# Copying x's pieces on GpSimd and taking more products straight from PSUM, in a fused long convolution and spectral mixing kernel

## The chip, the cores and the metric

The kernel runs on one core of a Trainium2 chip. A core has five engines with a queue of instructions each: TensorE for matmuls (PE in the profile, with its weight loads apart as PEld), VectorE (DVE), ScalarE (ACT), GpSimd (POOL) and SyncE (SP), which here only issues transfers. Each engine works through its own queue in order; engines wait for one another by semaphores. Matmuls write to PSUM, eight banks of 512 float32 a partition; DVE and ACT carry results from there to the on-chip memory SBUF. Transfers to and from DRAM are issued by SP or by GpSimd and done by 16 DMA engines.

The metric is the time of one execution in microseconds (us) on the device, the median of several runs. Lower is better.

## The reference

Two layers, one after the other, on x of shape (8, 5696, 128): batch, sequence, channels.

```python
# layer 1: causal long convolution along the sequence, by FFT
L = 2 * S
y = irfft(rfft(x, n=L, axis=1) * rfft(h, n=L, axis=0)[None], n=L, axis=1)[:, :S]
# layer 2: 64 Fourier modes of y, mixed over channels by a complex matrix per mode
X = rfft(y, axis=1)[:, :64]
Yr = einsum('bmd,mde->bme', X.real, w_r) - einsum('bmd,mde->bme', X.imag, w_i)
Yi = einsum('bmd,mde->bme', X.real, w_i) + einsum('bmd,mde->bme', X.imag, w_r)
u = y + irfft(Yr + 1j * Yi, n=S, axis=1)     # the other modes are zero
out = u + relu(u @ w_ch)
```

Inputs and output are float32; the kernel works in float16 with float32 sums in PSUM.

## The kernel before

The transforms are matmuls with fixed matrices. The sequence of 5696 is split as 89 x 64 (`NQ`, `J`). The batch is taken as four **pairs** of two; `g_` (0 to 3) counts them.

**Where x comes in.** A pair's x comes in eight pieces (`i`, 0 to 7: four for each batch entry). `x_load` issues two transfers for a piece from GpSimd's queue; they turn float32 into float16 and land in a staging tile, `Xr` for pair 0 and `Xt` for the others. `x_place` then copies the piece on DVE into `Xin` (L356), whose rows of 128 numbers stand 130 apart: 89 partitions, 16 rows of 128. `Xt` lies over the front of `As`, of which ticks already done are free.

**First transform.** `a_tile` j (0 to 31) multiplies four columns of `Xin` by the matrix `F` and evacuates the result into `As`, on DVE (L314) or ACT (L310). It needs all eight pieces. Tiles 0 to 5 of the next pair are done in the last ticks of the present one (table `border`), the rest between pairs. In that stretch GpSimd also issues the `wscr` transfers, which rearrange the mixing weights in DRAM.

**Ticks.** There are 90 frequencies, four to a tick, so 23 ticks (t = 0 to 22) a pair, and three more in which later steps run out. At each tick:

- `second`: 16 matmuls of `As` by `M` give the spectrum of x in two PSUM banks, one for each batch entry. `slot_of` says which of two slots of two banks. In pairs 1 to 3 the matmuls of an odd tick and of the next even one stand together (`twin`).
- `products`: DVE multiplies the spectrum by the spectrum of h, in `Hs`, into one of three `U` buffers (L592). In most ticks ACT first copies the spectrum from PSUM to `Xs` (`copied`, L308) and DVE reads `Xs`; in **straight** ticks DVE reads PSUM itself and there is no copy. Before the change the straight ticks are t = 3, 7, 11, 15, 19 of pairs 1 to 3; tick 0 has a form of its own (L584).
- Two ticks later four matmuls of `U` by `Wc` give Z; ACT casts it to `Zs` or `Zt`, two casts a tick (L308), and SP sends it to DRAM (`zscr`).
- A tick after that, eight matmuls of Z by `G` add to the 64 modes of layer 2.

In pair 0 the ticks to t = 16 also make the spectrum of h for tick t + 6 (`filter_tick`): matmuls, an evacuation to `Hs` on DVE (L312), and two transfers from SP that bring its halves to the other partitions.

**What sets the order.** Every instruction is recorded in the order in which the Python code calls for it; `Recorder` derives the waits from the tokens that an instruction reads and writes. There is no other planner, so an engine's queue is the order of the calls. At each tick `tick` calls first `x_place` for the pieces that the table `XPLACE` names, then `second` and `products`, then at even ticks 2 to 16 `x_load` of piece t/2 - 1 of the next pair (after the product of that tick), then the U matmuls, the casts and the G matmuls. The pieces are placed at ticks 9, 10, 12, 15, 16, 18, 20, 22 of pair 0 and 9, 10, 13, 14, 17, 18, 20, 22 of pairs 1 and 2, all on DVE.

**After the pairs** the modes are mixed (weights `W`), and the last stage, about a third of the time, brings convolution and modes back to the sequence (`UT`), multiplies by `w_ch` and writes the output. `reflect` (L505 on DVE) fills the second half of two of its matrices, `S4a` and `IBs`; memsets on GpSimd (L493) clear parts of the tiles that Z comes back to.

Of the kernel before, what the change touches and what calls it, by code (L numbers as in the profile page):

```python
# [7 lines left out]
U32 = mybir.dt.uint32  # L8
# [115 lines left out]
def bass_long_conv_fft__then__afno_spectral_mix_kernel(nc, x, h, moe_w_r, moe_w_i, moe_w_ch, out):  # L124
    B, S, D = x.shape
# [3 lines left out]
    NQ = S // J  # L129
# [3 lines left out]
    NP = B // 2  # L133
# [72 lines left out]
    def at(name, cols, dt, off):  # L206
        return nc.alloc_sbuf_tensor_at(name, [P, cols], dt, offset=off)
# [10 lines left out]
    XS = D + 2  # L218
    XW = 2 * J * XS
    a_x = take(XW * 2)  # L220
    x_sb = at("Xin", XW, F16, a_x)
# [7 lines left out]
    NU, NXS, NZ, NZX = 3, 2, 6, 10  # L229
# [8 lines left out]
    XN = J // XC  # L238
    XB = XN * D
    x_raw = [at(f"Xr{i}", XB, F16, a_h + 2 * XB * i) for i in range(2 * XC)]  # L240
    x_st = [at(f"Xt{i}", XB, F16, a_as + i * XB * 2) for i in range(2 * XC)]
    u_s = [at(f"U{i}", 2048, F16, a_st + i * 4096) for i in range(NU)]
    x_s = [at(f"Xs{i}", 1024, F16, a_st + NU * 4096 + i * 2048) for i in range(NXS)]
    z_s = [at(f"Zs{i}", 1024, F16, a_st + NU * 4096 + (NXS + i) * 2048) for i in range(NZ)] + \
# [47 lines left out]
    R = Recorder(nc)  # L292
# [39 lines left out]
    def turns(name, items):  # L332
        i = ring2.get(name, 0)
        ring2[name] = i + 1
        return items[i % len(items)]
# [19 lines left out]
    def x_place(i, src, toks):  # L355
        R.add("vector", lambda e: e.tensor_copy(bass.AP(x_sb, i * XN * XS, [[XW, NQ], [XS, XN], [1, D]]),  # L356
                                                bass.AP(src, 0, [[XB, NQ], [D, XN], [1, D]])),
              list(toks) + XZ, [("xin", i)])

    def w_pieces():  # L360
# [13 lines left out]
    XZ = [("xz",)]  # L374
# [20 lines left out]
    XSLOT = [0, 2]  # L395
# [13 lines left out]
    for j in range(16):  # L409
        t = turns("h", [0, 2, 4])  # L410
# [126 lines left out]
    def with_h_at(g_, t):  # L537
        return g_ == 0 and t + LH < NT
# [3 lines left out]
    def copied(g_, t, sl):  # L542
        n = len(ticks[t])
        e = onchip[(g_, t)] = turns("e", list(range(NXS)))
        evac(bass.AP(x_s[e], 0, [[1024, P], [512, 2], [1, n * D]]), pv(sl, 0, [[512, 2], [1, n * D]]), [bank(sl), bank(sl + 1)],
             [("xs", e)], eng="scalar")
        return e

    def twin(g_, t):
        return g_ > 0 and t % 2 == 1  # L550

    def straight(g_, t):
        return g_ > 0 and t % 4 == 3

    def slot_of(g_, t):
        if g_ == 0 or t == 0:
            return XSLOT[(t + 1) % 2 if t and not with_h_at(g_, t) else 0]
        return XSLOT[((t - 1) // 4 + t) % 2]

    def second(g_, t):  # L560
        sl = slot_of(g_, t)
        for i, k in enumerate(ticks[t]):
            for r in range(2):
                for b in range(2):
                    col = k * 3 * J + (J if r == 0 else 0) + b * J
                    mm(pv(sl + b, i * D, [[1, D]]),
                       ap(m_sb, MW, J * b, J, col, [[1, P]]),
                       ap(a_sb, AW, J * b, J, (2 * k + r) * D, [[1, D]]), r == 0, r == 1,
                       AST + mtok(k), [bank(sl + b)])

    def products(g_, t, sl):
        n = len(ticks[t])
        bk = [bank(sl), bank(sl + 1)]
        i = t % NU
        hv = bass.AP(h_sb, KT * t * D, [[2 * HW, P], [HW, 2], [0, 2], [1, n * D]])
        uv = bass.AP(u_s[i], 0, [[2048, P], [1024, 2], [512, 2], [1, n * D]])
        src = pv(sl, 0, [[0, 2], [512, 2], [1, n * D]])
        if t == 0:
            e = turns("e", list(range(NXS)))
            evac(bass.AP(x_s[e], 512, [[1024, P], [1, n * D]]), pv(sl + 1, 0, [[1, n * D]]), [bank(sl + 1)], [("xs", e)], eng="scalar")  # L580
            hv = bass.AP(h_sb, 0, [[2 * HW, P], [HW, 2], [1, n * D]])
            for b, s_, tok, done in ((0, pv(sl, 0, [[0, 2], [1, n * D]]), bank(sl), ("u", i)),
                                     (1, bass.AP(x_s[e], 512, [[1024, P], [0, 2], [1, n * D]]), ("xs", e), ("u0", i))):
                R.add("vector", lambda e, b=b, s_=s_: e.tensor_tensor(bass.AP(u_s[i], b * 512, [[2048, P], [1024, 2], [1, n * D]]), s_, hv, MULT),  # L584
                      [tok, ("h", t, 0), ("h", t, 1, 0), ("h", t, 1, J)], [done])
            return
        if not straight(g_, t):
            e = onchip.get((g_, t))
            if e is None:
                e = copied(g_, t, sl)  # L590
            src, bk = bass.AP(x_s[e], 0, [[1024, P], [0, 2], [512, 2], [1, n * D]]), [("xs", e)]
        R.add("vector", lambda e: e.tensor_tensor(uv, src, hv, MULT),  # L592
              bk + [("h", t, 0), ("h", t, 1, 0), ("h", t, 1, J)], [("u", i)])

    Z_OLD = [("ag", k) for k in range(NS, NS + 8 * (NZX - NZ))]
    XPLACE = [9, 10, 12, 15, 16, 18, 20, 22], [9, 10, 13, 14, 17, 18, 20, 22]

    def zroom(g_, s_):
        return (s_ - 2 * NZ) % NZX if g_ == 0 and s_ >= 2 * NZ else s_ % NZS[g_]

    def xtok(n):
        return [("xt", n, p_) for p_ in range(2)]

    def tick(g_, t):
        if g_ + 1 < NP:
            for i in range(2 * XC):
                if t == XPLACE[g_ > 0][i]:
                    x_place(i, x_st[i], xtok(i))
        with_h = with_h_at(g_, t)
        if t < NT:  # L610
            of_two = t > 0 and twin(g_, t - 1)
            if not of_two:
                second(g_, t)
            products(g_, t, slot_of(g_, t))
            if twin(g_, t):
                second(g_, t + 1)
                if straight(g_, t):
                    copied(g_, t + 1, slot_of(g_, t + 1))
        drain = list(border[t]) if t in border and g_ + 1 < NP else []
        if drain and t >= NT:  # L620
            j, sl, e = drain.pop(0)
            a_tile(j, [sl], e)
        if g_ + 1 < NP and t % 2 == 0 and 0 < t <= 4 * XC:
            i = t // 2 - 1
            x_load(g_ + 1, i, x_st[i], xtok(i), [("u", t % NU)] + AST)
        if LC <= t < NT + LC:
            s_ = t - LC
            n = len(ticks[s_])
            i, zi = s_ % NU, zroom(g_, s_)
            zb = [turns("z", ZBANK) for b in range(2)]  # L630
            for b in range(2):
                for r in range(2):
                    mm(pv(zb[b], 0, [[1, n * D]]), (W1, W2)[r], u_s[i][:, r * 1024 + b * 512:r * 1024 + b * 512 + n * D],
                       r == 0, r == 1, [("u", i), ("wc",)] + ([("u0", i)] if s_ == 0 and b else []), [bank(zb[b])])
                evac(bass.AP(z_s[zi], b * D, [[1024, P], [2 * D, n], [1, D]]),
                     pv(zb[b], 0, [[D, n], [1, D]]), [bank(zb[b])], [("zs", zi, b)], eng="scalar",
                     after=once(("zx", zi, b), Z_OLD) if zi >= NZ else ())
            zo = (g_ * NK + KT * s_) * P * 256
            dma("sync", bass.AP(zs, zo, [[256, P], [P * 256, n], [1, 256]]),
                bass.AP(z_s[zi], 0, [[1024, P], [256, n], [1, 256]]), "z",  # L640
                [("zs", zi, 0), ("zs", zi, 1)], [("zd", g_, s_)])
            if drain and t >= NT:
                j, sl, e = drain.pop(0)
                a_tile(j, [sl], e)
        if LM <= t < NT + LM:
            s_ = t - LM
            zi = zroom(g_, s_)
            for b in range(2):
                for i, k in sorted(enumerate(ticks[s_]), key=lambda q: (s_ > 0 or q[1] != 1, q)):
                    if k % 2:  # L650
                        o, off, n, sl = pv(MB, b * P, [[1, P]]), (k + 1) // 2 * P, P, (k + 1) // 2
                    else:
                        ms, off = even[k]
                        n, sl = 2 * len(ms), 0
                        dims = [[M, 2]] if len(ms) == 1 else [[ms[1] - ms[0], 2], [M, 2]]
                        o = pv(MB, b * P + ms[0], dims)
                    mm(o, z_s[zi][:, i * 256 + b * P:i * 256 + b * P + P], g_sb[:, off:off + n],
                       k == 1 and b == 0, k == NK - 1 and b == 1, [("g", sl // GP), ("zs", zi, b)], [bank(MB)])
        if drain and t < NT + LM - 1:
            j, sl, e = drain.pop(0)  # L660
            a_tile(j, [sl], e)
        if with_h:
            filter_tick(t + LH, [2, 3])
# [167 lines left out]
    for g_ in range(NP):  # L831
        last = g_ == NP - 1
        order = [(c_, b) for b in range(2) for c_ in range(NCH)] if last else [(c_, b) for c_ in range(NCH) for b in range(2)]
        for n, (c_, b) in enumerate(order):
            i = NCH * g_ + c_
# [44 lines left out]
```

## Time and profile before

| | |
|---|---|
| median of 3 runs (lowest, highest) | 387.9 us (386.63, 389.21) |
| span of the profiled execution, first to last instruction | 383.2 us |
| what lies around that span, by the median | 4.7 us |
| granted TensorE clock | 0.995 of full speed |
| PE busy | 364.4 us, 95% of the span |
| DVE busy | 312.2 us, 81% |
| ACT busy | 302.2 us, 79% |
| POOL busy | 83.0 us, 22% |

The profile is of one execution; its own time is given as the span alone. The ticks of pair 0 lie at about 45 to 94 us, of pair 1 at 110 to 149, of pair 2 at 166 to 204, of pair 3 at 221 to 260; the stretches between are the first transform of the next pair.

Busy time counts from an instruction's start to its end. Neighbours on an engine overlap by some 0.08 us, so the spacing of starts tells more than durations. A matmul's end is modelled; its start is not. A wait is put down to the event that came last before the instruction; where that engine had long been done, it was another.

### The profile page before, as it was taken

The page shows a single profiled execution, that of the slowest core. Times are in us where ns is not written, and L with a number is a line of the kernel's source. Part 1 is how long each engine was busy: PE and PEld are TensorE (multiplying, and loading weights), DVE is VectorE, ACT ScalarE, POOL GpSimd, SP SyncE. Part 2 cuts the span into 40 slices and gives each one's busy share as a digit, 9 for nine tenths or more (in the row PEclk, how much of TensorE's full clock was granted, in tenths as well). Part 3 has the DMA queues.
Part 4 walks back from the last instruction along what each step waited for, and adds up shares of the span by engine and source line. Part 5 has one row for each costly group of instructions (what it writes and reads, how often), then busy time and mean ns, then how long its engine had stood idle before and what let it go on. Part 6 is the DMA issues. An engine that isn't in the chain of part 4 may idle for free.

```text
span 383.2 us, 12579 instructions
## 1 busy us (share of the span) xinstructions
PE 364.4 (95%) x5396; PEld 284.9 (74%) x5396; DVE 312.2 (81%) x349; ACT 302.2 (79%) x486; POOL 83.0 (22%) x133
## 2 busy tenths in 40 slices
PE   7999999998989999989998989999999999999994
PEld 7997766665866666866666856668898988988873
DVE  6878888997998999998998987885437677767876
ACT  1268689898889997989997989996457676777785
POOL 8400013220453320643220511219400000000000
PEclk9999999999999999999999999999899999999999
DMA  7998559999699999899996839999999999999978
GB/s 147 197 284 329 142 107 268 282 239 296 93 138 198 216 249 252 93 133 198 257 248 193 87 113 364 328 357 388 404 400 398 406 417 401 409 415 380 376 290 355
DMA packets 86865, 103.94 MB, mean 271 GB/s; under 512 B 22638, under 2 KB 72430, under 8 KB 83330
## 3 DMA queue, kind: packets, MB, share of 16 engines
q1 hardware_dynamic: 62523, 67.73, 50.6%
q0 software_dynamic: 24288, 35.43, 43.9%
q8 instruction: 42, 0.69, 0.7%
q14 instruction: 12, 0.10, 0.1%
HBM read 70.61 MB, written 51.12 MB: 318 GB/s over the span
## 4 chain that ended last, share of the span: by engine, by line
PE 73%; DMA 10%; DVE 6%; ACT 5%; POOL 3%; issue 2%; SPq 0%; DVEq 0%; POOLq 0%
PE ps L320 73%; DMA Xr<-in_x_dram 4%; DMA Xt<-in_x_dram 4%; DVE As L314 2%; POOL Xr L317 2%; ACT As L310 2%; DVE U L584 1%; ACT R L814 1%; DMA Hs<-Hs 1%; ACT UT L308 1%; DVE Xin L356 1%; ACT Zs L308 1%; DVE UT L312 0%; DVE O L815 0%; DVE Hs L312 0%
## 5 line engine op out<-in xcount | busy, mean ns | idle before, releaser
L592 DVE TENSOR_TENSOR U<-Xs,Hs 128x2048 f16<-128x2048 f16 (+1 forms) x73 | 86.7, 1191 | 14.3 <-ACT Xs L308 11.2
L320 PE MATMUL ps<-U,Wc 128*128 128x512 f16 (+1 forms) x368 | 94.0, 376 | 0.6 <-DVE U L592 0.6
L308 ACT CAST Xs<-ps 128x1024 f16<-128x1024 f32 (+1 forms) x77 | 74.8, 976 | 11.3 <-PE ps L320 8.7
L308 ACT CAST Zs<-ps 128x512 f16<-128x512 f32 (+1 forms) x134 | 70.6, 596 | 2.7 <-PE ps L320 2.3
L815 DVE TENSOR_TENSOR O<-ps,R 128x512 f32<-128x512 f32 x81 | 52.5, 685 | 19.8 <-ACT R L814 13.1
L314 DVE TENSOR_SCALAR As<-ps 128x720 f16<-128x720 f32 x70 | 58.1, 885 | 5.8 <-PE ps L320 5.0
L814 ACT ACTIVATE R<-ps 128x512 f32<-128x512 f32 x96 | 50.9, 572 | 14.5 <-PE ps L320 14.1
L320 PE MATMUL ps<-F,Xin 128*128 128x180 f16 x512 | 53.9, 250 | 4.2 <-DVE Xin L356 1.7
L320 PEld LDWEIGHTS ps<-F,Xin 128*128 128x128 f16 x512 | 44.5, 155 | 12.8 <-DVE As L314 3.7
L320 PE MATMUL ps<-As,M 64*128 64x128 f16 x1440 | 50.4, 217 | 3.5 <-DVE U L584 2.9
L310 ACT ACTIVATE As<-ps 128x720 f16<-128x720 f32 (+1 forms) x61 | 45.8, 770 | 8.7 <-PE ps L320 7.2
L320 PE MATMUL ps<-WI,UT 128*128 128x256 f16 x360 | 51.7, 278 | 0.5 <-DVE O L815 0.4
L320 PEld LDWEIGHTS ps<-U,Wc 128*128 128x128 f16 x368 | 28.5, 97 | 29.4 <-ACT Zs L308 4.7
L317 POOL DMA_DIRECT2D Xt<-in_x_dram x48 | 25.9, 545 | 104.6 <-PE ps L320 100.7
L320 PEld LDWEIGHTS ps<-As,M 64*128 64x128 f16 x1440 | 40.6, 94 | 8.8 <-DVE U L584 3.6
L308 ACT CAST UT<-ps 128x712 f16<-128x712 f32 x40 | 30.0, 752 | 17.2 <-PE ps L320 16.2
L320 PEld LDWEIGHTS ps<-WI,UT 128*128 128x128 f16 x360 | 39.2, 152 | 4.1 <-issue 1.9
L320 PE MATMUL ps<-IBs,C 128*128 128x356 f16 x128 | 39.7, 319 | 0.8 <-ACT UT L308 0.3
L320 PEld LDWEIGHTS ps<-G,Zs 128*128 128x128 f16 x524 | 28.9, 96 | 14.0
L592 DVE TENSOR_TENSOR U<-ps,Hs 128x2048 f16<-128x2048 f32 x15 | 34.2, 2283 | 0.0
L320 PE MATMUL ps<-G,Zs 128*128 128x128 f16 (+2 forms) x524 | 32.4, 191 | 0.0
L320 PE MATMUL ps<-F 128*128 128x180 f16 x284 | 28.2, 255 | 2.6 <-DMA F<-cF 2.6
(87 smaller groups left out, 506.0 us busy)
## 6 DMA issues: line engine op xcount, KB each, us to landing
out_dram<-O SPq DMA_DIRECT2D x39, 512.0 KB, 10.8
zscr<-Zs SPq DMA_DIRECT2D x64, 256.0 KB, 6.9
Xt<-in_x_dram POOLq DMA_DIRECT2D x24, 320.0 KB, 7.0
zscr<-Zt SPq DMA_DIRECT2D x24, 256.0 KB, 7.2
W<-wscr POOLq DMA_DIRECT2D x4, 1024.0 KB, 8.3
M<-cM POOLq DMA_DIRECT2D x5, 720.0 KB, 20.5
ZT0a<-zscr SPq DMA_DIRECT2D x3, 1024.0 KB, 13.5
Hs<-Hs SPq DMA_DIRECT2D x44, 64.0 KB, 5.4
```

The lines of the kernel that those rows point to most:

```text
L308: R.add(e, lambda h_: h_.copy(dst, src), reads, writes, after=after)
L310: R.add(e, lambda h_: h_.activation(dst, src, COPY, scale=scale), reads, writes, after=after)
L314: R.add(e, lambda h_: h_.tensor_scalar_mul(dst, src, scale), reads, writes, after=after)
L317: R.add(eng, lambda h_: h_.dma_start(dst, src), reads, writes, ring=ring, after=after)
L320: R.add("tensor", lambda h_: h_.matmul(o, l, r, start=st, stop=sp), reads, writes)
L356: R.add("vector", lambda e: e.tensor_copy(bass.AP(x_sb, i * XN * XS, [[XW, NQ], [XS, XN], [1, D]]), bass.AP(src, 0, [[XB, NQ], [D, XN], [1 ...
L584: R.add("vector", lambda e, b=b, s_=s_: e.tensor_tensor(bass.AP(u_s[i], b * 512, [[2048, P], [1024, 2], [1, n * D]]), s_, hv, MULT), [tok, ...
L592: R.add("vector", lambda e: e.tensor_tensor(uv, src, hv, MULT), bk + [("h", t, 0), ("h", t, 1, 0), ("h", t, 1, J)], [("u", i)])
L814: R.add("scalar", lambda e: e.activation(rv, src_r, RELU), bk, [("r", i % NR)], after=once(("r", i % NR), G_ALL + XTT + [("y", 0), ("y", 1 ...
L815: R.add("vector", lambda e: e.tensor_tensor(ov, src_u, rv, ADD), bk + [("r", i % NR)], [key + (h_,)], after=once(key, old))
```

## The change

Two things. First, 20 of the 24 copies from `Xt` to `Xin` move from DVE to GpSimd: the last four of pair 0 and all eight of pairs 1 and 2. They copy the same bytes as 32-bit words, 64 to a row instead of 128 halves. They stand at straight ticks, two to a tick, and wait, beside the piece's landing, for the product of the tick before (the token `("u", (t - 1) % NU)`). Second, the straight ticks become a table: 17, 19 and 21 in pair 0, which had none, and 3, 5, 9, 11, 15, 17, 19, 21 in pairs 1 to 3. `slot_of` counts PSUM slots by the new table. TensorE's and SP's instructions and their order stay; ACT loses 12 of its `Xs` copies.

```diff
+    x_32 = x_sb[:, :].bitcast(U32).tensor
+    xt_32 = [t_[:, :].bitcast(U32).tensor for t_ in x_st]
...
+    def x_place32(i, toks):
+        R.add("gpsimd", lambda e: e.tensor_copy(bass.AP(x_32, i * XN * XS // 2, [[XW // 2, NQ], [XS // 2, XN], [1, D // 2]]),
+                                                bass.AP(xt_32[i], 0, [[XB // 2, NQ], [D // 2, XN], [1, D // 2]])),
+              list(toks) + XZ, [("xin", i)])
...
+    STRAIGHT = [(17, 19, 21)] + [(3, 5, 9, 11, 15, 17, 19, 21)] * (NP - 1)
+
     def straight(g_, t):
-        return g_ > 0 and t % 4 == 3
+        return t in STRAIGHT[g_]
...
     def slot_of(g_, t):
         if g_ == 0 or t == 0:
             return XSLOT[(t + 1) % 2 if t and not with_h_at(g_, t) else 0]
-        return XSLOT[((t - 1) // 4 + t) % 2]
+        n = 1
+        for i in range(2, t + 1):
+            n ^= not straight(g_, i - 2)
+        return XSLOT[n]
...
-    XPLACE = [9, 10, 12, 15, 16, 18, 20, 22], [9, 10, 13, 14, 17, 18, 20, 22]
+    XPLACE = [9, 10, 12, 15, 17, 17, 21, 21], [11, 11, 15, 15, 17, 17, 21, 21]
...
                 if t == XPLACE[g_ > 0][i]:
-                    x_place(i, x_st[i], xtok(i))
+                    if straight(g_, t):
+                        x_place32(i, xtok(i) + [("u", (t - 1) % NU)])
+                    else:
+                        x_place(i, x_st[i], xtok(i))
```

## The prediction

> **What bounds the kernel now.** I read the costliest groups first, for the price of what is moved, then busy time by stretch, to see which engine has room, then the timelines of single engines, for what PE really waits for. Of each group: count, busy time, mean ns of one, idle time before it and its releaser.
>
> ```profile
> L592 DVE TENSOR_TENSOR U<-Xs,Hs 128x2048 f16<-128x2048 f16 (+1 forms) x73 | 86.7, 1191 | 14.3 <-ACT Xs L308 11.2
> L308 ACT CAST Xs<-ps 128x1024 f16<-128x1024 f32 (+1 forms) x77 | 74.8, 976 | 11.3 <-PE ps L320 8.7
> L592 DVE TENSOR_TENSOR U<-ps,Hs 128x2048 f16<-128x2048 f32 x15 | 34.2, 2283 | 0.0
> ```
> ```profile
> L356 DVE COPY Xin<-Xt 89x2048 f16<-89x2048 f16 x24 | 16.4, 682 | 0.8 <-DMA Xt<-in_x_dram 0.8
> ```
>
> A product from PSUM saves ACT a copy and costs DVE about twice as much. Starts follow closer than durations: in the timeline a straight product holds DVE for 2.20 us, one from Xs for 1.14, a placing copy for 0.60.
>
> Next, four ticks of pair 2 (two copies on DVE) and of pair 3 (none); the columns are the stretch, its length, then busy time of PE, PEld, DVE, ACT and POOL.
>
> ```profile
> 180.00:187.00 7.00, 7.00 (x118) 4.63 (x114) 6.89 (x7) 6.89 (x12) 2.08 (x4) 1.00 1.04 214
> 235.00:242.00 7.00, 7.00 (x120) 4.63 (x116) 5.78 (x5) 6.89 (x12) 0.53 (x1) 1.00 1.09 395
> ```
>
> Without the copies DVE is 1.1 us less busy, and the four ticks still take 7.0 us. So DVE is not the bound. ACT at 6.89 could be, or PE. PE's timeline in pair 3 decides it:
>
> ```profile
> 231.05 1.07 PE L320 MATMUL ps<-As,M 64*128 64x128 f16 x32
> ...
> 233.25 1.07 PE L320 MATMUL ps<-U,Wc 128*128 128x512 f16 x4
> ...
> 234.58 1.07 PE L320 MATMUL ps<-As,M 64*128 64x128 f16 x32
> ...
> 236.78 1.02 PE L320 MATMUL ps<-U,Wc 128*128 128x512 f16 x4
> ...
> 238.06 1.07 PE L320 MATMUL ps<-As,M 64*128 64x128 f16 x32
> ```
>
> Two ticks take 3.53 us, the next two 3.48. The first holds PE's only wait (1.07 against 1.02: a weight load waits for ACT's Zs); in the second matmuls follow without a gap. **PE is the bound**, and ACT costs it 0.05 us in four ticks: five times a pair, 0.25 us a pair.
>
> The larger waits lie where a pair ends:
>
> ```profile
> 138.25 1.21 DVE L592 TENSOR_TENSOR U<-Xs,Hs 128x2048 f16<-128x2048 f16 x1
> ...
> 148.18 0.69 DVE L356 COPY Xin<-Xt 89x2048 f16<-89x2048 f16 x1 [0.17 <-DMA Xt<-in_x_dram]
> ```
> ```profile
> 140.00 1.04 POOL L317 DMA_DIRECT2D Xt<-in_x_dram  x2 [2.29 <-PE ps L320]
> ```
> ```profile
> 148.93 0.85 PE L320 MATMUL ps<-F,Xin 128*128 128x180 f16 x8 [0.64 <-DVE Xin L356]
> ```
>
> Tick 16's product ends at 139.46, GpSimd issues piece 7 0.54 later (the PE named as releaser was long done), it lands at about 148.15, DVE copies it, and PE has waited 0.64 us. Pair 2 shows 0.65 in the same place and pair 0 0.40.
>
> **The change, part by part.** It moves 4 + 8 + 8 copies of pairs 0, 1 and 2 to GpSimd and makes 3 products of each pair straight, 12 in all. *ACT* loses 12 Xs copies of 0.98, 11.8 us. This is worth PE's 0.05 us waits alone: at most 0.25 in each of three pairs. *DVE* loses 20 copies of 0.60, 12.0 us, and gains 12 times 2.20 - 1.14, 12.7 us. Where straight and copied products alternate, two ticks take DVE 2.20 + 1.14 = 3.34 of PE's 3.48: it fits, with 0.1 to spare, and ticks 7 and 13, copied ones, give back 1.1 each. *PSUM*: a straight product keeps its banks 2.20 us; they are written again 3.48 us later, so nothing waits there.
>
> *GpSimd* gains 20 copies of 1024 words, which no row shows. Its memsets of 2048 words take 1.82, so 0.91 for writing as many; that is my nearest row. From below, DVE's own copy at 0.68; from above, 1.82, if a word read and written costs twice a word written. I take 0.95. By the Trainium skill (GPSIMD Engine Reference, "Performance versus the Vector engine") simple bodies take 1.03 cycles a word at 1.2 GHz, an estimate of 0.88, but its measured tight loop 1.8, an estimate of 1.54; the first leaves my sum, the second would give about 398.
>
> *When the copies run.* They wait for the product of the tick before, so as to lie beside the straight one. But in GpSimd's queue the pieces 4, 6 and 7, issued after the products of ticks 10, 14 and 16, stand right ahead of the copies of ticks 11, 15 and 17. Each takes 0.53 to start and 1.04 for its two transfers. So these copies start 1.57 after the straight product and end at 1.57 + 1.90 = 3.47, and the product ends at 2.20. The rest, 1.27, lies beside the next product, from Xs and Hs. Only the copies of tick 21 have no load ahead and fit. What such an overlap costs, the nearest rows show, DVE's and then GpSimd's:
>
> ```profile
> 262.30 3.61 DVE L505 TENSOR_SCALAR S4a<-S4a,SG 128x2759 f16<-128x2759 f16 x1
> ...
> 269.40 0.93 DVE L505 TENSOR_SCALAR IBs<-IBs,SG 128x2759 f16<-128x2759 f16 x1
> ```
> ```profile
> 261.60 1.82 POOL L493 MEMSET ZT1b<- 32x2048 uint32 x1
> 263.35 1.82 POOL L493 MEMSET ZT2b<- 32x2048 uint32 x1
> ```
>
> The same DVE instruction takes 0.93 alone and 3.61 beside two memsets: it ends 0.74 after the second, and did not get in between them. A product from Xs and Hs is no such instruction, so its cost lies between 0 and the whole 1.27; I take 1.27, since it too works from SBUF to SBUF. The Trainium skill (SBUF — State Buffer, "Who interferes with whom") says that a DVE instruction with two SBUF inputs contends with a GpSimd one that reads SBUF, and one with a single SBUF input does not. By that rule the next product is held and the straight one is free; by a reading of the row in which only that kind of instruction is held, the sum would be 386.3. No product in this trace meets a GpSimd read.
>
> *The sum for pairs 1 and 2.* Let e be the end of tick 17's first matmuls (138.4 in pair 1). Unhindered, DVE ends product 16 at e - 0.1. Between a straight tick's first matmuls and its U matmuls PE has 0.5 + 0.87 + 0.33 + 0.87 + 0.42 + 1.0 = 4.0 us of other blocks (their starts in PE's timeline), and DVE needs 2.25: a delay under about 1.8 costs nothing, and the same holds a tick later (5.2 against 3.4). Tick 11's 1.27 is made good at ticks 13 and 14. Tick 15's makes product 16 end at e + 1.05, which is where it ends now (139.46), so piece 7 lands when it does now. Tick 17 adds its 1.27: product 18 is 2.4 late, over 1.8 by 0.55, and PE waits that long. Products 19 and 20 follow, ending at e + 9.1; copies 6 and 7 at e + 9.1 + 0.1 + 1.9 = e + 11.1, where PE can start on Xin; now it starts at e + 10.5 (148.93). Product 22 ends at e + 11.9, now e + 11.05, and the first As evacuation behind it frees PE's next banks. So +0.6 to +0.85, less 0.2 of ACT waits: **+0.6 a pair**.
>
> *Pair 0.* Product 20 starts at 90.47, with h just landed (its transfers, issued by SP, are not moved). Then straight 21 to about 93.8, product 22 to 94.4 (now 94.06), copies 6 and 7 to 93.8 (Xin is ready at 93.5 now): +0.4. The copies of tick 17 delay product 18, which has 1.41 idle behind it. *Pair 3* has no copies: -0.25. Behind the copies of tick 21 in GpSimd's queue stand the wscr writes, which wait for As evacuations 6 us later (100.32, 155.73): nothing.
>
> Sum 0.4 + 0.6 + 0.6 - 0.25 = +1.35. The profiled execution spans 383.2, the median of the timed runs is 387.9, so 4.7 lies around the span and stays; **389.2 us**.
>
> **The rivals.** *Products are not held* by a copying GpSimd, or get in between two copies. Then product 16 ends near e - 0.1 and piece 7 is issued at 138.85 and lands, at 8.15, by 147.0; copy 7 ends at 148.0 and PE's 0.65 goes. Three times -0.25, twice -0.65, +0.4 in pair 0: -1.6, so 386.3. For it: no row shows a product held. Against: the 3.61. Even if all PE waits of the four pairs went, with pair 0's 0.56 and 0.40, I count 3.0 us: the gain cannot pass 0.8%.
> *Copies are slow*: from 1.15 us on, the delay of three groups passes PE's 1.8 already at tick 15. At 1.3, each group holds DVE 1.57 + 2.6 - 2.2 = 1.97, PE waits 0.2, 0.8 and 1.9 us at the three, and 0.3 more at the end: 3.2 a pair, 0.8 in pair 0: +7, so 395. For it: the copy reads as well, in rows of 64. Against: the memset's rate.
> *The straight product is held too*, since Hs comes from SBUF: each of four groups costs 1.9, about 2.7 a pair, 393.4. Against: the one beside a memset at 246.67 took its 2.28, though that memset reads nothing.
>
> **Chances.** Forecast 0.45, not held 0.25, slow copies 0.20, straight held 0.07, else 0.03. A measurement of this kernel tells about 1% from no change, 384.0 to 391.8. Slower: 0.20 + 0.07 + 0.05 of the forecast, 0.32; faster 0.05, from the tail of the first rival; within 0.63. The range, 386.0 to 395.5, runs from the first rival to slow copies of 1.3; beyond it lie copies near 1.8 above and the capped gain below.
>
> **What would show it.** Copies on GpSimd near 0.95; products of ticks 12, 16 and 18 at 2 us or more instead of 1.22 in pairs 1 and 2; copies of ticks 11, 15 and 17 starting 1.6 us behind the product before; ACT near 290 us busy; PE waiting about 0.5 for a U at ticks 18 to 20, and 0.6 to 1.2 where a pair ends. Products at 1.22 throughout would prove the first rival; copies over 1.15 the second; straight products over 2.28 beside copies the third. The prediction is wrong, too, if piece 7 lands at another delay than 8.15, since PE at the end of pairs 1 and 2 waits for it.

## The result, and the profile after

The changed kernel takes 392.62 us (median of 4 runs, 392.41 to 394.1), the kernel before 388.33 (386.63 to 389.21, 4 runs). The ratio is 1.0121, 95% interval 1.0085 to 1.0157: **slower by 1.2%**. The forecast was 389.2 in a range of 386.0 to 395.5; slower was the right sign, but the likeliest class, within 1%, had 0.63, and slower by over 1% had 0.32.

The profiled span grew from 383.2 to 390.7 us. Cut where PE begins on a pair's first `a_tile`, and last where it begins to mix the modes, it divides so (us):

| stretch | before | changed | |
|---|---|---|---|
| to the first tile of pair 0 | 27.9 | 27.9 | 0 |
| pair 0 | 65.6 | 66.4 | +0.7 |
| pair 1 | 55.4 | 57.3 | +1.9 |
| pair 2 | 55.3 | 57.8 | +2.5 |
| pair 3 | 58.2 | 58.1 | -0.15 |
| from the mixing to the end | 120.7 | 123.3 | +2.6 |

The last stretch holds no line of the change, and in the profiles of this study it takes 120.7 to 123.5 us, whatever was edited; in the changed kernel one transfer (`ZT0b`) landed 16.6 us after its issue there. Pair 0, with its old code, took 65.6, 65.6 and 66.4 us in three profiles. So the span's 7.5 us overstate the change. The 4.4 us of pairs 1 and 2 are its own, and the medians differ by 4.3. The profiled execution of the kernel before was also a short one: in its timed runs 2.1 us lie between span and time (387.89 against 385.8), in the changed kernel's 1.85 (392.55 against 390.7). So of the 4.7 us above some 2.6 are not around the span at all, but the amount by which that one execution was shorter than the median; the forecast, which is the median plus 1.35, is not touched by this.

The costliest groups of the changed kernel (busy time, mean ns of one, idle time before it), and the form that is new:

```profile
L604 DVE TENSOR_TENSOR U<-Xs,Hs 128x2048 f16<-128x2048 f16 (+1 forms) x61 | 80.7, 1325 | 11.4 <-ACT Xs L310 8.9
L310 ACT CAST Xs<-ps 128x1024 f16<-128x1024 f32 (+1 forms) x65 | 62.2, 962 | 20.8 <-PE ps L322 19.3
...
L604 DVE TENSOR_TENSOR U<-ps,Hs 128x2048 f16<-128x2048 f32 x27 | 61.6, 2283 | 0.4 <-DMA Hs<-Hs 0.4
```
```profile
L363 POOL COPY Xin<-Xt 89x1024 uint32<-89x1024 uint32 x20 | 20.3, 1047 | 15.2 <-DVE U L604 15.2
```

ACT lost its 12 copies and now waits 19.3 us for PE before its Xs copies, where it was 8.7. Straight products keep their 2283 ns, but a product from Xs went from 1191 to 1325 ns in the mean: some are longer. A GpSimd copy takes 1.05 us. The stretches of four ticks say where the loss lies; the columns are the stretch, its length and the busy time of PE, PEld, DVE, ACT and POOL:

```profile
198.00:205.00 7.00, 5.63 (x78) 3.47 (x75) 7.00 (x4) 4.89 (x10) 3.07 (x4) 1.00 1.09 253
240.00:247.00 7.00, 7.00 (x118) 4.50 (x112) 7.00 (x5) 6.44 (x12) 0.53 (x1) 1.00 1.09 384
```

In pair 3, without copies, PE still issues 118 matmuls in 7 us. Late in pair 2 it issues 78, and DVE is busy throughout. The timelines of GpSimd and of DVE in pair 1 show why, at ticks 15 to 17:

```profile
137.11 1.04 POOL L319 DMA_DIRECT2D Xt<-in_x_dram  x2 [1.48 <-PE ps L322]
138.15 2.03 POOL L363 COPY Xin<-Xt 89x1024 uint32<-89x1024 uint32 x2
141.80 1.04 POOL L319 DMA_DIRECT2D Xt<-in_x_dram  x2 [1.62 <-DVE U L604]
142.83 2.03 POOL L363 COPY Xin<-Xt 89x1024 uint32<-89x1024 uint32 x2
149.34 2.02 POOL L363 COPY Xin<-Xt 89x1024 uint32<-89x1024 uint32 x2 [4.48 <-DVE U L604]
```
```profile
136.50 2.28 DVE L604 TENSOR_TENSOR U<-ps,Hs 128x2048 f16<-128x2048 f32 x1
138.70 2.56 DVE L604 TENSOR_TENSOR U<-Xs,Hs 128x2048 f16<-128x2048 f16 x1
141.18 2.28 DVE L604 TENSOR_TENSOR U<-ps,Hs 128x2048 f16<-128x2048 f32 x1
143.38 2.56 DVE L604 TENSOR_TENSOR U<-Xs,Hs 128x2048 f16<-128x2048 f16 x1
```

The straight product of tick 15 starts at 136.50; a piece's load holds GpSimd's queue until 138.15, 1.65 us later; the two copies then run to 140.18, and the next product, from Xs and Hs, ends at 141.26, 1.1 us behind them. It takes 2.56 us instead of 1.22: it is *held*, which here means that it has started but does its work only behind the copies. The copies of tick 21 (149.34), with no load ahead, lie beside their straight product. PE's timeline shows what the delay costs:

```profile
143.52 0.62 PE L322 MATMUL ps<-As,M 64*128 64x128 f16 x16 [0.29 <-DVE U L604]
144.07 1.04 PE L322 MATMUL ps<-U,Wc 128*128 128x512 f16 x4
144.95 0.49 PE L322 MATMUL ps<-G,Zt 128*128 128x4 f16 x8
146.00 1.04 PE L322 MATMUL ps<-U,Wc 128*128 128x512 f16 x4 [0.57 <-DVE U L604]
146.87 0.49 PE L322 MATMUL ps<-G,Zt 128*128 128x4 f16 x8
147.29 0.62 PE L322 MATMUL ps<-As,M 64*128 64x128 f16 x16
148.20 0.40 PE L322 MATMUL ps<-As,M 64*128 64x128 f16 x8 [0.29 <-DVE U L604]
...
151.53 0.85 PE L322 MATMUL ps<-F,Xin 128*128 128x180 f16 x8 [0.45 <-DVE U L604]
```

Two kinds of wait are new: U matmuls wait for a late product, and matmuls of `As` wait for a straight product that still reads their PSUM banks. From the starts of all 768 matmuls of a pair, the gaps ahead of U matmuls grew by 1.20 us in pair 1 and 1.70 in pair 2, those between matmuls of `As` by 0.85 and 0.93, and the wait at the pair's end shrank by 0.18 in each: 1.87 and 2.45, all but 0.04 us of the loss.

### The profile page after: what moved, and what is told of

It is laid out like the page before. It is cut to its first block, busy times and chain, and to the rows that moved or that the text cites. A ratio compares the mean times of both kernels' runs of the same rounds, so it can differ in the third digit from the quotient of the medians.

```text
span 390.7 us, 12555 instructions
## 1 busy us (share of the span) xinstructions
PE 365.9 (94%) x5396; PEld 284.2 (73%) x5396; DVE 321.2 (82%) x329; ACT 292.2 (75%) x474; POOL 102.6 (26%) x153
## 4 chain that ended last, share of the span: by engine, by line
PE 56%; DVE 14%; DMA 13%; ACT 8%; issue 4%; POOL 2%; SPq 1%; DVEq 0%; POOLq 0%
PE ps L322 56%; DVE U L604 8%; DMA Xr<-in_x_dram 4%; DMA ZT0b<-zscr 4%; DMA Hs<-Hs 4%; DVE As L316 2%; POOL Xr L319 2%; ACT As L312 2%; ACT Zs L310 1%; ACT Xs L310 1%; DVE U L596 1%; ACT R L829 1%; DMA zscr<-Zs 1%; ACT Zt L310 1%; ACT UT L310 1%
## 5 line engine op out<-in xcount | busy, mean ns | idle before, releaser
L604 DVE TENSOR_TENSOR U<-Xs,Hs 128x2048 f16<-128x2048 f16 (+1 forms) x61 | 80.7, 1325 | 11.4 <-ACT Xs L310 8.9
L310 ACT CAST Xs<-ps 128x1024 f16<-128x1024 f32 (+1 forms) x65 | 62.2, 962 | 20.8 <-PE ps L322 19.3
L316 DVE TENSOR_SCALAR As<-ps 128x720 f16<-128x720 f32 x70 | 58.1, 886 | 5.8 <-PE ps L322 5.0
L604 DVE TENSOR_TENSOR U<-ps,Hs 128x2048 f16<-128x2048 f32 x27 | 61.6, 2283 | 0.4 <-DMA Hs<-Hs 0.4
```

The source lines that it names most:

```text
L310: R.add(e, lambda h_: h_.copy(dst, src), reads, writes, after=after)
L316: R.add(e, lambda h_: h_.tensor_scalar_mul(dst, src, scale), reads, writes, after=after)
```

## The experiments

All against the kernel before; the medians of its runs in the two series are 387.89 and 387.90. The columns of pairs are cut as above, in us of the profiled span.

| run | median, us | ratio (95%) | pair 0 | 1 | 2 | 3 |
|---|---|---|---|---|---|---|
| before | 387.9 | | 65.6 | 55.4 | 55.3 | 58.2 |
| changed | 392.62 | 1.0121 (1.0085 to 1.0157) | 66.4 | 57.3 | 57.8 | 58.1 |
| e1_copies_first | 386.42 | 0.9956 (0.9927 to 0.9985) | 65.5 | 54.6 | 54.6 | 58.1 |
| e2_cf_pair0_old | 385.77 | 0.9946 (0.9914 to 0.9977) | 65.6 | 54.6 | 54.6 | 58.1 |
| e3_copies_behind | 396.36 | 1.0215 (1.0152 to 1.0279) | 71.1 | 57.5 | 58.8 | 59.4 |
| e4_one_row | 386.23 | 0.9951 (0.9916 to 0.9986) | 65.9 | 54.6 | 54.9 | 58.1 |
| e5_before_one_row | 385.59 | 0.9935 (0.9913 to 0.9957) | 65.5 | 54.5 | 54.6 | 58.4 |
| e6_table_alone | 395.13 | 1.0204 (1.0168 to 1.0241) | 67.3 | 57.8 | 57.8 | 58.1 |
| e7_pair0_alone | 387.10 | 0.9991 (0.9969 to 1.0013) | 66.9 | 55.0 | 55.5 | 58.2 |
| e8_before_early_loads | 386.71 | 0.9974 (0.9953 to 0.9995) | 66.4 | 55.0 | 55.0 | 58.2 |

### The load moved behind the copies

```diff
-        if g_ + 1 < NP and t % 2 == 0 and 0 < t <= 4 * XC:
-            i = t // 2 - 1
-            x_load(g_ + 1, i, x_st[i], xtok(i), [("u", t % NU)] + AST)
+        if g_ + 1 < NP and t % 2 == (g_ > 0) and 0 < t <= 4 * XC:
+            i = (t - 1) // 2
+            x_load(g_ + 1, i, x_st[i], xtok(i), ([] if g_ else [("u", t % NU)]) + AST)
```

> The changed kernel, but in pairs 1 and 2 a piece of the next pair is issued at the odd tick before, behind that tick's copies in GpSimd's queue, and waits for the tick's first matmuls instead of its product. So no load stands ahead of a copy, and copies should start about 0.1 us behind the product before and lie beside the straight one. Theory (a copy that reads SBUF holds a product with both inputs in SBUF, and the load ahead pushes the copy there): products of ticks 12, 16 and 18 back at 1.22 us, the copies still 1.05 each; pairs 1 and 2 give back their 1.9 and 2.5 us and a little at their ends, pair 0 keeps its 0.7: 387.5 to 389 us, near the kernel before. Rival (the table of straight products is what costs: DVE without slack and PSUM banks held longer): 391 us or more, with DVE's U products still late. Rival (the landing of the last piece is what PE waits for): 390, with PE's wait at the pair's end gone and the waits at ticks 16 to 20 left.

Its GpSimd and DVE timelines at ticks 14 to 16 of pair 1, and PE's at the pair's end:

```profile
135.89 2.02 POOL L363 COPY Xin<-Xt 89x1024 uint32<-89x1024 uint32 x2 [2.62 <-DVE U L604]
137.85 1.03 POOL L319 DMA_DIRECT2D Xt<-in_x_dram  x2
```
```profile
134.60 1.22 DVE L604 TENSOR_TENSOR U<-Xs,Hs 128x2048 f16<-128x2048 f16 x1 [0.75 <-ACT Xs L310]
135.74 2.28 DVE L604 TENSOR_TENSOR U<-ps,Hs 128x2048 f16<-128x2048 f32 x1
137.94 1.21 DVE L604 TENSOR_TENSOR U<-Xs,Hs 128x2048 f16<-128x2048 f16 x1
```
```profile
148.09 0.84 PE L322 MATMUL ps<-F,Xin 128*128 128x180 f16 x8
```

The copies start 0.15 us behind the straight product and end with it; the next product takes 1.21. Nothing else of the change is undone, and pairs 1 and 2 give back 2.7 and 3.2 us. That is more than they lost, as PE now goes from tick to pair's end without a wait. The run is faster than both kernels, below what was expected. The theory holds. The rival that the table alone costs falls for this order of the queue, and so does the one by which only the landing of the last piece counts (390). The edit also makes the pieces land earlier; what that is worth by itself is asked further down, of the kernel before. One product in pair 0, where the load still stands ahead, is held (2.03 us), inside an idle stretch.

### The same, with pair 0 as before

```diff
-    STRAIGHT = [(17, 19, 21)] + [(3, 5, 9, 11, 15, 17, 19, 21)] * (NP - 1)
+    STRAIGHT = [()] + [(3, 5, 9, 11, 15, 17, 19, 21)] * (NP - 1)
...
-    XPLACE = [9, 10, 12, 15, 17, 17, 21, 21], [11, 11, 15, 15, 17, 17, 21, 21]
+    XPLACE = [9, 10, 12, 15, 16, 18, 20, 22], [11, 11, 15, 15, 17, 17, 21, 21]
```

> As e1_copies_first, and pair 0 as in the kernel before: no straight products there, its eight copies on DVE at the old ticks. Theory: the 0.7 us that pair 0 lost goes as well, 386.5 to 388.5, at or a little below the kernel before; as PE is the bound with about 1 us of waits a pair, no more than 2 us below it. Rival (the table of straight products costs): 390.5 or more.

0.9946, the best ratio of the kernels that compute everything, but its interval overlaps that of the run above, and pair 0 took 65.6 against 65.5 us. The 0.7 us of pair 0 did not show up as a gain; e7 asks for them again.

### Copies behind the straight product

```diff
-                    if straight(g_, t):
-                        x_place32(i, xtok(i) + [("u", (t - 1) % NU)])
-                    else:
+                    if not straight(g_, t):
                         x_place(i, x_st[i], xtok(i))
...
             products(g_, t, slot_of(g_, t))
+            for i in range(2 * XC):
+                if g_ + 1 < NP and straight(g_, t) and t == XPLACE[g_ > 0][i]:
+                    x_place32(i, xtok(i) + [("u", t % NU)])
```

> The changed kernel with the suspected cost doubled: each pair of copies waits for the straight product itself, not for the one before it, so that both copies lie wholly beside the next product, from Xs and Hs. Theory (held): the product behind each of the four groups takes 1.22 + about 2.0 instead of up to 2.56, group 21's holds the last product too; 0.7 us more for each of three groups and 2 for the last, some 3 to 4 us a pair in pairs 1 and 2 and 1 to 2 in pair 0: 399 to 403 us. Rival (copies hold nothing and the table costs): products at the same lengths as in the changed kernel, 392 to 394 with only the end of a pair later.

Slower still, but not in the way that was expected. GpSimd and DVE at ticks 12 to 14 of pair 1:

```profile
136.64 3.94 POOL L363 COPY Xin<-Xt 89x1024 uint32<-89x1024 uint32 x2 [0.69 <-DVE U L604]
```
```profile
136.49 1.21 DVE L604 TENSOR_TENSOR U<-Xs,Hs 128x2048 f16<-128x2048 f16 x1
138.39 1.29 DVE L604 TENSOR_TENSOR U<-Xs,Hs 128x2048 f16<-128x2048 f16 x1 [0.69 <-ACT Xs L310]
140.71 1.23 DVE L604 TENSOR_TENSOR U<-Xs,Hs 128x2048 f16<-128x2048 f16 x1 [1.03 <-POOL Xin L363]
```

The product starts 0.15 us before the first copy, and now the *copies* are held: two take 3.94 us instead of 2.03, the products 1.21 and 1.29, and only the third waits, 1.03 us. So the hold works both ways. The first copy was held by a product that had started 0.15 us earlier; and the product at 138.39, which started 0.15 us before the second copy, did its work before it, although the first copy still ran until 138.60.

Against the changed kernel pair 1 loses 0.2 us, not the 3 to 4 expected. The other pairs say little, as the granted clock was lower there. In pair 0 (71.1) PE ran for 10 us at 0.66 of its clock, the seventh number here (between POOL's busy time and the DMA share):

```profile
90.00:100.00 10.00, 7.71 (x67) 4.61 (x68) 7.27 (x5) 5.24 (x9) 2.02 (x2) 0.66 0.63 186
```

In pairs 2 and 3 the clock was 0.97, and pair 3, which has no copies, took 59.4 us instead of 58.1; so pair 2's 1.0 us more can't be put down to the copies. Nor can all of the 2% of the time.

### GpSimd copies of one row

```diff
-        ... bass.AP(x_32, i * XN * XS // 2, [[XW // 2, NQ], [XS // 2, XN], [1, D // 2]]),
-            bass.AP(xt_32[i], 0, [[XB // 2, NQ], [D // 2, XN], [1, D // 2]])),
+        ... bass.AP(x_32, i * XN * XS // 2, [[XW // 2, NQ], [XS // 2, 1], [1, D // 2]]),
+            bass.AP(xt_32[i], 0, [[XB // 2, NQ], [D // 2, 1], [1, D // 2]])),
```

> The changed kernel with each GpSimd copy cut to one of its 16 rows, waits and places kept; the other rows of Xin are not written, so that part of the computation is left out. Theory (the copies' time beside the next product is the cost): the loads ahead stay, but the copies take some 0.1 us each and end before the straight product does; all products at 1.22, 387 to 388.5 us. Rival (the table costs): 391.5 or more, since the table is the same. Rival (the wait of GpSimd for the product before, in front of the loads, is the cost): 391 or more.

Durations of its copies, shortest, median and longest in ns:

```profile
L363 POOL COPY Xin<-Xt x20: 232/242/1257, 84.6 to 203.0; 89x64 uint32<-89x64 uint32 x20
```

With table, waits and loads ahead as in the changed kernel, and only the copies short, pairs 1 and 2 take what they take in e1 to 0.3 us, and the time is 386.23, below the 387 expected. So it is the copies' time beside the next product, not the table and not GpSimd's waits. The longest, 1.26 us, met a product that had started 0.11 us before it.

### The kernel before, with copies of one row

```diff
-    def x_place(i, src, toks):
-        R.add("vector", lambda e: e.tensor_copy(bass.AP(x_sb, i * XN * XS, [[XW, NQ], [XS, XN], [1, D]]),
-                                                bass.AP(src, 0, [[XB, NQ], [D, XN], [1, D]])),
+    def x_place(i, src, toks, rows=XN):
+        R.add("vector", lambda e: e.tensor_copy(bass.AP(x_sb, i * XN * XS, [[XW, NQ], [XS, rows], [1, D]]),
+                                                bass.AP(src, 0, [[XB, NQ], [D, rows], [1, D]])),
...
-                    x_place(i, x_st[i], xtok(i))
+                    x_place(i, x_st[i], xtok(i), 1)
```

> The kernel before, with each of the 24 DVE copies from Xt to Xin cut to one of its 16 rows, at its place and with its waits; the other rows are not written, so that part of the computation is left out. It asks what DVE's copies cost the kernel before at all. Theory (PE bounds the ticks, DVE has room): some 13 us of DVE's time go, and the time falls only by the copy behind the last piece's landing, about 0.5 us in each of three pairs, to 386 to 387.9. Rival (DVE bounds the ticks): the 24 copies, 0.6 each, come back as several us: under 383.

0.9935, 2.3 us by the medians, a little more than expected, and far from the rival's 5 us and over. A copy takes DVE 0.18 us here instead of 0.68, so 12.0 us of DVE's work are gone, and they are worth 0.9 and 0.7 us in pairs 1 and 2. With the loads where they are, moving these copies off DVE had little more to bring, and e1 and e2 gain as much.

### The table alone

```diff
-    XPLACE = [9, 10, 12, 15, 17, 17, 21, 21], [11, 11, 15, 15, 17, 17, 21, 21]
+    XPLACE = [9, 10, 12, 15, 16, 18, 20, 22], [9, 10, 13, 14, 17, 18, 20, 22]
...
-                    if straight(g_, t):
-                        x_place32(i, xtok(i) + [("u", (t - 1) % NU)])
-                    else:
-                        x_place(i, x_st[i], xtok(i))
+                    x_place(i, x_st[i], xtok(i))
```

> The changed kernel's table of straight products, with all 24 copies on DVE at the old ticks: one part of the change alone. DVE gains 12 times 1.06 us and loses nothing, and from tick 15 on it has 2.20 + 1.14 in two ticks of 3.48 and up to two copies of 0.60. Theory: DVE now falls behind by 0.5 to 1 us in every two of the last ticks; by tick 21 it is some 3 us late, more than the 1.8 that PE bears, and straight products hold PSUM banks that the next matmuls need: 1 to 2 us a pair in pairs 1 and 2, 0.5 to 1.5 in pair 0, 390.5 to 393. Rival (the table is free, since ACT is relieved): 387 to 388.5.

Worse than expected, 395.13. PE's timeline at the end of pair 1:

```profile
147.95 0.62 PE L322 MATMUL ps<-As,M 64*128 64x128 f16 x16
148.80 0.40 PE L322 MATMUL ps<-As,M 64*128 64x128 f16 x8 [0.23 <-DVE U L604]
...
153.33 0.85 PE L322 MATMUL ps<-F,Xin 128*128 128x180 f16 x8 [1.44 <-DVE Xin L358]
```

With products straight and copies on one engine, DVE is the bound from tick 9 on: matmuls of `As` wait for banks (1.3 and 1.4 us more between their starts than before, in pairs 1 and 2), and at the pair's end PE waits 1.44 us for the last copy instead of 0.64. Of the change's two parts, then, the table loses 2% by itself, and GpSimd's copies give back 0.6 to 0.8 (by the medians and by the ratios), badly placed as they are. The other part alone, GpSimd's copies with the old table, was not run; so it stays open whether the new table adds anything to e1 (386.42), when the old one with short copies takes 385.59 (e5).

### Pair 0 alone

```diff
-    STRAIGHT = [(17, 19, 21)] + [(3, 5, 9, 11, 15, 17, 19, 21)] * (NP - 1)
+    STRAIGHT = [(17, 19, 21)] + [(3, 7, 11, 15, 19)] * (NP - 1)
...
-    XPLACE = [9, 10, 12, 15, 17, 17, 21, 21], [11, 11, 15, 15, 17, 17, 21, 21]
+    XPLACE = [9, 10, 12, 15, 17, 17, 21, 21], [9, 10, 13, 14, 17, 18, 20, 22]
...
-                    if straight(g_, t):
+                    if g_ == 0 and straight(g_, t):
                         x_place32(i, xtok(i) + [("u", (t - 1) % NU)])
```

> The change made in pair 0 alone (straight products at ticks 17, 19, 21, last four copies on GpSimd), pairs 1 to 3 as in the kernel before. Theory (pair 0's 0.7 us come from the straight product of tick 21, which ends later behind a landing of h): 388.2 to 388.9, a ratio of 1.001 to 1.003. Rival (pair 0's end moves with the landing of h from run to run and the change costs nothing there, as in the run with the copies first, where its end stood where it was): ratio 0.998 to 1.001.

0.9991, interval 0.9969 to 1.0013: no cost that can be measured, as the rival had it. The profile has 66.9 us for pair 0, but 66.4 occur with its old code (e8). Whether the change costs pair 0 some tenths stays open.

### The kernel before, with earlier loads

```diff
-        if g_ + 1 < NP and t % 2 == 0 and 0 < t <= 4 * XC:
-            i = t // 2 - 1
-            x_load(g_ + 1, i, x_st[i], xtok(i), [("u", t % NU)] + AST)
+        if g_ + 1 < NP and t % 2 == (g_ > 0) and 0 < t <= 4 * XC:
+            i = (t - 1) // 2
+            x_load(g_ + 1, i, x_st[i], xtok(i), ([] if g_ else [("u", t % NU)]) + AST)
```

> The kernel before with the one edit of the copies-first run and nothing of the change: in pairs 1 and 2 a piece is issued at the odd tick before, after that tick's first matmuls. It asks whose gain the copies-first run is. Theory (the earlier landing of piece 7 takes away PE's 0.65 us wait at the end of pairs 1 and 2, and GpSimd's copies are worth little): 386.3 to 387, a ratio of 0.996 to 0.998, most of what the copies-first run gained. Rival (the gain comes from taking the copies off DVE): piece 7 lands earlier, but DVE reaches its copy no sooner, 387.5 to 388.3.

0.9974: a gain without any of the change, as large as expected. PE at the end of pair 1:

```profile
149.57 0.85 PE L320 MATMUL ps<-F,Xin 128*128 128x180 f16 x8 [0.35 <-DVE Xin L356]
```

The wait went from 0.64 to 0.35, not to 0: the piece has landed, but DVE still has its last copy to do. In e1 it is 0. So of the 0.8 and 0.7 us that e1 gains in pairs 1 and 2, about half (0.4 and 0.3) is the earlier load and half the rest of the edit. Some 0.3 us of the gain of e8's time, and of that of e1 and e2, lie outside the profiled span: between span and time there are 1.8 us in the mean of their runs, and 2.1 in the kernel before. No run shows why.

## Why the prediction was right or wrong

**The bound: right.** Relieving ACT of three copies, 2.9 us, brought 0.15 us in pair 3, where nothing else changed (forecast 0.25), and freeing DVE of three quarters of its copies' time is worth under 1 us a pair (e5).

**The copy's price: right.** 1.05 us against 0.95. The Trainium skill's rate for simple bodies (GPSIMD Engine Reference, "Performance versus the Vector engine"), an estimate of 0.88, is near it; the 1.54 from its measured loop is not borne out. The rival of slow copies, from 1.15 us on, did not come about.

**The load ahead, and the hold: right.** The copies start 1.65 us behind the straight product (forecast 1.57), and hold the next one 2.56 - 1.22 = 1.34 us (1.27), at ticks 12, 16 and 18 as named. Straight products stay at 2.28 us beside copies. So the rivals that nothing is held and that straight products are held too both fall. The Trainium skill (SBUF — State Buffer, "SBUF: two separate sides") has it so: between a DVE instruction with two SBUF inputs and a GpSimd one that reads SBUF, whichever starts first keeps the shared pair of ports for its whole length. These runs agree that the product is held (2.56), in e3 the copy (1.97 and 2.03 us for 1.05), and that straight products, with one SBUF input, stay at 2.28 beside copies. They differ in one point: at tick 16 the product starts at 138.70, 0.43 us before the second copy (139.13), and that copy still goes first.

**The sum for pairs 1 and 2: wrong in size.** Forecast +0.6 each, measured +1.9 and +2.5. The mechanism came about; three terms of the sum were too small.

- "Unhindered, DVE ends product 16 at e - 0.1" was too early. In e1, where nothing holds it, the next product starts at 139.08, and e is 138.42 there: e + 0.66. The copied ticks, which were to be slack, are bound by ACT: products 7 and 8 wait 0.75 and 0.73 us for Xs copies in both runs, and in e1 products 13 and 14 wait 0.67 and 0.75. So DVE enters a straight tick late in any case: tick 11's product starts 0.65 us after its matmuls (129.29 against 128.64; 0.65 in e1 too). "Tick 11's 1.27 is made good at ticks 13 and 14" was right for DVE: tick 15's product starts 25.27 us after the pair's first one in both runs (136.50 - 111.23, and 135.74 - 110.47 in e1). But PE did pay for it: the U matmuls of tick 12 wait 0.30 us. So product 16 ends at 0.66 (e1) + 1.34 (the hold) - 0.30 (PE's own delay) = 1.70 behind e (141.18; e is 139.48 in the changed kernel), not 1.05. The U matmuls of ticks 12, 16 and 18 together wait 1.2 us in pair 1 and 1.7 in pair 2 where I had 0.55, at tick 18 alone.
- "PSUM: nothing waits there" was worked out for a product on time and not again for a late one. The straight product of tick 17 ends at 143.46, 4.0 us after its matmuls instead of 2.25, and the next matmuls into its banks, due 3.6 after, wait. The trace has 0.85 and 0.93 us for such waits in pairs 1 and 2.
- Pair 2's further 0.5 us is one product of 3.05 us, at tick 18, because the copies beside it came later:

```profile
200.10 0.53 POOL L319 DMA_DIRECT2D Xt<-in_x_dram  x1 [0.48 <-issue]
```
```profile
200.69 3.05 DVE L604 TENSOR_TENSOR U<-Xs,Hs 128x2048 f16<-128x2048 f16 x1
```

GpSimd issued the two transfers of piece 7 at 199.10 and 200.10, 0.48 us apart more than elsewhere. Such a gap stands in the kernel before as well (195.09 and 196.09); I had not counted it against the copies behind it.

**The pair's end: right in kind, wrong in place.** The loss was forecast there, as a wait of 0.6 to 1.2 us for the last copies. They do end late, at e + 11.9 (151.36) instead of e + 11.1, but PE, which had paid most of the delay in the waits above, waits only 0.45 us, less than the 0.64 before. Piece 7 landed 7.36 us after its issue instead of 8.15, still 0.12 ahead of product 20, so it did not set the end.

**Pair 0: not settled.** +0.4 was forecast; the profile has +0.7, the timed run of that part alone none. In the profile PSUM has a part here too: PE waits 1.12 us, at 90.18, for tick 19's straight product, which a landing of h had made late.

**The chances** followed from the pair's sum: with 1.9 and 2.5 in its place the same working gives 387.9 + 0.4 + 4.4 - 0.25 = 392.5. That 392.62 lies inside the range is in part luck: the upper part of the range stood there for slow copies, which did not come about.

## What to carry to other kernels

Work put beside a chosen neighbour runs beside it only if nothing stands ahead of it in its own queue: count what the queue issues at the same event, transfers included, before asking whether the lengths fit. When a delay is added, redo every "nothing waits" with the delayed times, the banks that the late instruction still reads among them. And look at what the neighbouring edit is worth without the change: here an earlier load alone made the old kernel 0.3% faster (interval 0.05 to 0.47%), and a reordered queue turned a loss of 1.2% into a gain of 0.4 to 0.5%.

## What the runs showed of the hardware

- Between two GpSimd copies issued one right behind the other, a waiting DVE product mostly did not get in: where it started 0.43 us before the second copy, it did its work after both (2.56 us, ending 1.1 us behind the second copy; five products of pairs 1 and 2, and a sixth at 0.91 us). Where it started 0.15 us (e3) or 0.11 us (e4) before the second copy, in the last 0.2 us of the first, it did get in: it took 1.29 and 1.28 us, and the second copy 2.03 instead of 1.05 and 1.26 instead of 0.23. What decides between the two stays open.
- Apart from that, the hold is paid by what starts second, and 0.15 us of a start are enough: product first, the copy takes 1.97 us instead of 1.05 (e3); copy first, the product takes 2.56 instead of 1.22.
- A GpSimd copy of 64 words a partition takes 0.24 us (median, e4), one of 1024 words, in 16 rows, 1.05: about 0.19 us fixed and 0.84 ns a word, by the difference.
